# The first batch of a fused attention and Fourier kernel: the keys' half of a pair's memory and its scores in turn, the values' half last

## The chip, the cores and the metric

The kernel runs on one core of one Trainium2 chip. The metric is the device time of one execution in microseconds (us); lower is better. Three runs of the kernel before took 980.9, 981.11 and 982.27 us, median 981.11. Besides there is one profiled execution, whose trace is read below. TensorE is PE in the views, VectorE is DVE, ScalarE is ACT, GpSimd is POOL, and SP is the engine that issues the DMAs.

## The reference

Inputs are q, k, v of 8 batches x 8 heads x 576 tokens x 64, phi of 8 x 8 x 576 x 32, and two feed-forward weights of 512 x 2048 and 2048 x 512. Cut to what matters:

```python
a = softmax(phi, axis=2)                      # pooling weights per token
k_m = einsum('bhsm,bhsd->bhmd', a, k)         # 32 key memories per head
v_m = einsum('bhsm,bhsd->bhmd', a, v)         # 32 value memories per head
attn = softmax(q @ k_m.T / 8)                 # scores of 576 tokens over 32 memories
x = (attn @ v_m), heads side by side          # 576 x 512 per batch
u = x + real(fft(fft(x, axis=1), axis=2))     # Fourier mix over tokens and features
un = (u - mean) / sqrt(var + 1e-6)
out = u + relu(un @ w_ch1) @ w_ch2
```

## The kernel before

Heads are handled in pairs, four pairs (`NG`) per batch. For a pair, `pair_memory` makes on TensorE the product of keys and pooling weights (columns 0 to 63 of a PSUM tile `pm`) and of values and pooling weights (columns 64 to 127); VectorE multiplies both by a mask `mk` into `kmf` (in `share`) and `vmf`. `pair_scores` multiplies queries by `kmf` into a PSUM tile `psc`, makes the softmax on VectorE with the exponential on ScalarE, and writes sums and differences of tokens as float16 high and low parts into `aeo` (the low part of the first rows, on VectorE, is marked `s{b}_{g}`). `values` takes the products of `vmf` with the feature cosines `vt` (PSUM tiles `pv`, result `vh`), and `spectrum` those of `aeo` with the token cosines `ct` (PSUM tiles `pa`, result `at`). `mix_m` (PSUM tile `pp_t`, lines L600 to L640) and `mix_x` (`px_t`, from the transposed attention `attnT`) give rows of u in `uring`; `norm_chunk` normalises them, transposes them on TensorE for the first chunk (`unring`), and the feed-forward follows in chunks of 256 rows, 17 in all, each of 8 parts (`NW`) of the weights. PSUM tiles of all these steps but the feed-forward's `ph` and `po` share a pool of four buffers (`psg`).

The first chunk is different: its weights arrive as 64-bit floats and are converted on chip while they are first used (`ffn1_direct` into `ph`, `ffn2_direct` into `po`, float32 matmuls). A conversion (`to_f32`) is one pass on ScalarE (L808) and on VectorE a shift (L810) and two fused passes (L811, L821). For the keys in the list `LP`, the last one is instead a shift on VectorE (L816) and an integer add on POOL (L819). `split_w1` then makes two float16 parts. A square with its sum (L830) gives a scale.

Order: a scheduler places the instructions of each engine by its own timeline, so program order is not the order on the engine. `issue_after` holds an instruction behind a marked one, where both are on one engine; `GATE1` and `GATE2` name the marks that hold the conversion of w1's and w2's eight parts. `un1` is VectorE's normalisation of the second tile, `uh0` ScalarE's copy into `unring`. `high_priority` lets the scheduler place an instruction earlier. All loads go through SP in the order of issue; parts of the first batch's pairs are in tiles that later hold something else (`stg`, `w2s`), and pair 2's keys and values share bytes with w2's first converted part. `keep_busy` runs matmuls on zeros to keep TensorE's clock up.

Of the kernel before, what the change touches and what calls it, by code (L numbers as in the profile page):

```python
# [10 lines left out]
F32 = mybir.dt.float32  # L11
# [5 lines left out]
ALU = mybir.AluOpType  # L17
# [23 lines left out]
STEPS = 2  # L41
NX = 2
KEEP = [8, 18, 0, 0, 22, 4, 3]
GATE1 = [[]] + [["un1", "uh0"]] * 7
GATE2 = [["un1", "uh0"]] * 8
NA = 2
NAH = 1
KP = [1]
# [3 lines left out]
UW = UB * DM  # L52
EB = 14
L2 = [2, 4, 6]
LP = ["2_0", "2_2", "2_4", "2_6"]
W1_STAGE = ["w4", "w6", "s1", "w6", "s1", "s2", "s1", "x"]
W2_STAGE = ["b10", "b14", "s2", "b10", "b14", "x", "s2", "s1"]

# [74 lines left out]
def kernel(  # L133
# [72 lines left out]
    def tiny(tag, n, bufs=2):  # L206
        if tag not in rings:
            rings[tag] = [taken[0], 0]
            taken[0] += n * bufs
        o, i = rings[tag]  # L210
        rings[tag][1] += 1
        o += i % bufs * n
        assert taken[0] <= 400, taken
        return scratch[:, o : o + n]
# [52 lines left out]
    def groups():  # L267

        last = [None]

        def mm(out, lhsT, rhs, start, stop):
            with tc.issue_after(last[0].ins) if start and last[0] is not None else nullcontext():
                m = nc.tensor.matmul(out, lhsT=lhsT, rhs=rhs, start=start, stop=stop)  # L273
            if stop:
                last[0] = marks["pe"] = m

        return mm
# [56 lines left out]
    def pooling_weights(b):  # L334
# [28 lines left out]
        for g in range(2):  # L363
# [6 lines left out]
                et[:, g].rearrange("p l t c -> p (l t) c"), elt.rearrange("p l c -> p (l c)"), False, f"et_{b}_{g}"  # L370
            )

    def pair_memory(b, g, r, vmf, ivs):

        n = f"{b}_{g}"
        kv = r[:, :KV].rearrange("p (t w c) -> p t w c", t=NST, w=2)
        q = r[:, KV:]
        if b < NX:
            pm = psg.tile([P, 512], F32, tag="g", name=f"pm_{n}")
            mm = groups()  # L380
            for w in range(2):
                for t in range(NST):
                    mm(
                        pm[:, w * 64 : w * 64 + 64],
                        lhsT=kv[:, t, w, :],
                        rhs=et32[:, g // 2, t, 64 * (g % 2) : 64 * (g % 2) + 64],
                        start=(t == 0),
                        stop=(t == NST - 1),
                    )
            kmf = share[:, g * 64 : g * 64 + 64] if b == 0 else tiny("kmf", 64, 2)  # L390
            nc.vector.tensor_tensor(out=kmf, in0=pm[:, 0:64], in1=mk[:, 0:64], op=ALU.mult)
            nc.vector.tensor_tensor(
                out=vmf[:, g],
                in0=pm[:, 64:128].unsqueeze(1).to_broadcast([P, 2, 64]),
                in1=mk[:, 0:64].unsqueeze(1).to_broadcast([P, 2, 64]),
                op=ALU.mult,
            )
            return q, None, kmf, 1.0 / 8.0
        am = tiny("am", 3, 1)
        for w in range(2):  # L400
            nc.scalar.activation(
# [490 lines left out]
    def background():  # L892
# [3 lines left out]
        for b in range(B):  # L896
# [5 lines left out]
            pooling_weights(b)  # L902
            yield (nt if half_made is None else half_made), 0
            if b == 0:
                for g in range(NG):
                    mem[g] = pair_memory(b, g, first[g], vmf, ivs)
            for step in range(NG + 2):
                if step < NG and b > 0:
                    r = load_pair(b, step)
                if step >= 2 and b > 0:  # L910
                    pair_transpose(b, step - 2, ahl.pop(step - 2), attnT)
                if 0 <= step - 1 < NG:
                    ahl[step - 1] = pair_scores(b, step - 1, *mem.pop(step - 1), aeo)
                    yield (nt if half_made is None else half_made), 0
                if step < NG and b > 0:
                    mem[step] = pair_memory(b, step, r, vmf, ivs)
                    yield (nt if half_made is None else half_made), 0
            vbd, vh, isg, igx, isq = values(b, vmf, ivs)
# [30 lines left out]
        while True:  # L949
            yield n_tiles, 0  # L950

    nc.sync.dma_start(out=mk, in_=mk_d)
    load_phi(0)
    keep_busy(KEEP[0])
    first = [load_pair(0, 0)]
# [145 lines left out]
```

## Time and profile before

| quantity | value |
|---|---|
| median of 3 runs | 981.11 us |
| profiled execution, device time | 980.04 us |
| its span in the trace | 978.2 us |
| TensorE busy in the span | 937.8 us |
| VectorE busy in the span | 570.7 us |

The span begins with the first instruction and ends with the last; the device time also has 1.84 us around it. The page gives busy times and groups of instructions; the timeline gives instructions in order of time, merged where they follow one another (count behind the x), with the idle time in front in brackets; a window is a stretch of time with each engine's busy time in it. A row of matmuls in float32 counts each matmul twice.

### The profile page before, as it was taken

Reading aid. Unit: us, or ns where it says so; the run is one execution under the profiler, and the core shown is the slowest. Engines: PE = TensorE matmul, PEld = TensorE weight load, DVE = VectorE, ACT = ScalarE, POOL = GpSimd, SP = SyncE. Lnnn points to the kernel's source line nnn. Section 1 sums busy time; section 2 is a strip of 40 time slices with the busy share of each in tenths; the row PEclk is TensorE's granted clock in tenths of the full one; section 3 lists DMA queues with packets and bytes.
Section 4 is the critical chain, followed back from the end, with each engine's and each line's share of the span. In section 5 each row is a group of like instructions: output and inputs, shape, how many; then the busy total and the mean of one; then the engine's idle time right before and its main releaser. Section 6 shows DMA issues by size and latency. Waiting matters only on the chain.

```text
span 978.2 us, 18885 instructions
## 1 busy us (share of the span) xinstructions
PE 937.8 (96%) x7753; PEld 664.3 (68%) x7753; DVE 570.7 (58%) x1301; ACT 456.0 (47%) x910; POOL 229.9 (23%) x249
## 2 busy tenths in 40 slices
PE   9388898989999999999999999999999999999998
PEld 6256577666687667676767776767677667666664
DVE  3889958757655765776623666657655765311111
ACT  2455448695555544755431645565545543401110
POOL 1213324334221422333120223123311321300000
PEclk9699999999999999999999999999999999999999
DMA  9706564064225430465111632164214310210000
GB/s 351 282 7 265 180 173 131 1 140 122 62 50 99 116 88 29 88 127 122 39 23 36 122 107 68 44 120 122 69 44 86 79 26 29 44 44 1 23 22 22
DMA packets 115959, 88.08 MB, mean 90 GB/s; under 512 B 100385, under 2 KB 100385, under 8 KB 113825
## 3 DMA queue, kind: packets, MB, share of 16 engines
q1 hardware_dynamic: 115872, 86.87, 34.0%
q8 instruction: 61, 1.00, 0.5%
q14 instruction: 26, 0.20, 0.1%
HBM read 58.15 MB, written 9.44 MB: 69 GB/s over the span
## 4 chain that ended last, share of the span: by engine, by line
PE 82%; DVE 8%; ACT 4%; DMA 2%; issue 2%; POOL 1%; SPq 0%; DVEq 0%; POOLq 0%; ACTq 0%
PE po L765 34%; PE ph L273 33%; PE pm L273 4%; PE pp_t L273 3%; PE psc L273 2%; PE px_t L273 1%; PE pa L585 1%; DVE w1t L821 1%; DVE w2s L811 1%; PE po L729 1%; POOL scratch L678 1%; DMA rawt<-in_raw 1%; PE pf L343 1%; DVE w1t L811 1%; DVE uring L654 0%
## 5 line engine op out<-in xcount | busy, mean ns | idle before, releaser
L273 PE MATMUL ph<-unring,w1t 128*128 128x256 f16 x3264 | 389.0, 273 | 2.7 <-DMA unring<-ud 2.7
L765 PE MATMUL po<-w2s,hring 128*128 128x512 f16 x1632 | 378.6, 379 | 0.0
L273 PEld LDWEIGHTS <-w1t 128*128 128x128 f16 x3264 | 314.6, 98 | 65.8 <-DMA unring<-ud 3.2
L765 PEld LDWEIGHTS <-hring 128*128 128x128 f16 x1632 | 156.6, 98 | 158.0 <-issue 0.4
L756 DVE SCALAR_TENSOR_TENSOR hring<-ph,hring 128x512 f16<-128x512 f32 x136 | 93.0, 685 | 154.7 <-ACT hring L755 154.3
L755 ACT ACTIVATE hring<-ph 128x512 f16<-128x512 f32 x136 | 80.2, 590 | 168.3 <-PE ph L273 167.9
L501 POOL TENSOR_TENSOR aring<-aring,scratch 128x384 f32<-128x384 f32 x28 | 24.4, 870 | 202.2 <-DVE scratch L499 201.3
L678 POOL TENSOR_TENSOR scratch<-scratch,small 128x1 f32<-128x1 f32 x36 | 25.0, 700 | 155.6 <-DVE scratch L677 132.1
L273 PEld LDWEIGHTS <-stg 128*128 128x128 f16 x1152 | 44.9, 98 | 10.3 <-POOL stg L418 1.3
L495 ACT ACTIVATE aring<-aring,scratch 128x384 f32<-128x384 f32 x24 | 14.7, 612 | 70.4 <-DVE aring L494 70.4
L699 POOL TENSOR_TENSOR ud<-un,ud 128x1024 f16<-128x1024 f32 x17 | 37.5, 2203 | 29.9 <-ACT ud L698 29.9
L273 PE MATMUL pp_t<-vh,at 128*128 128x255 f16 (+3 forms) x288 | 36.6, 273 | 2.4 <-ACT at L600 1.5
L273 PE MATMUL pm<-et,stg 128*128 128x64 f16 (+1 forms) x780 | 37.0, 199 | 1.3 <-POOL stg L418 1.2
L418 POOL TENSOR_TENSOR stg<-rawt,stg 128x640 f16<-128x640 f32 x12 | 17.8, 1487 | 81.9 <-ACT rawt L417 81.9
L485 DVE TENSOR_REDUCE scratch<-psc 128x12 f32<-128x384 f32 x32 | 17.7, 552 | 32.6 <-PE psc L273 17.5
L640 DVE SCALAR_TENSOR_TENSOR share<-pp_t,scratch,small 128x257 f32<-128x257 f32 (+1 forms) x48 | 21.1, 480 | 25.3 <-ACT small L637 25.3
L729 PE MATMUL po<-w2s,hring 128*128 128x512 f32 x64 | 30.3, 600 | 4.8 <-ACT hring L715 2.9
L520 ACT CAST aeo<-eo 128x384 f16<-128x384 f32 x30 | 15.3, 511 | 41.4 <-DVE eo L517 41.2
L513 DVE TENSOR_TENSOR eo<-aring 128x128 f32<-128x128 f32 x29 | 30.8, 1063 | 5.6 <-POOL aring L511 5.6
L654 DVE SCALAR_TENSOR_TENSOR uring<-px_t,scratch,share 128x256 f32<-128x256 f32 (+1 forms) x80 | 33.9, 475 | 0.2
L777 DVE SCALAR_TENSOR_TENSOR uring<-po,small,uring 128x512 f32<-128x512 f32 x34 | 24.0, 741 | 16.5 <-PE po L765 16.5
L511 POOL TENSOR_TENSOR aring<-aring 128x128 f32<-128x128 f32 x56 | 32.7, 603 | 2.1
(240 smaller groups left out, 1232.6 us busy)
## 6 DMA issues: line engine op xcount, KB each, us to landing
rawt<-in_raw SPq DMA_DIRECT2D x15, 640.0 KB, 5.1
stg<-in_raw SPq DMA_DIRECT2D x15, 640.0 KB, 4.1
out<-uring SPq DMA_DIRECT2D x36, 256.0 KB, 2.3
stg<-in_w SPq DMA_DIRECT2D x7, 1024.0 KB, 5.7
rawt<-in_raw SPq DMA_DIRECT2D x15, 384.0 KB, 3.1
stg<-in_raw SPq DMA_DIRECT2D x15, 384.0 KB, 3.1
phs<-in_raw SPq DMA_DIRECT2D x32, 160.0 KB, 5.2
w2s<-in_w SPq DMA_DIRECT2D x4, 1024.0 KB, 9.8
```

The source lines that it names most:

```text
L273: m = nc.tensor.matmul(out, lhsT=lhsT, rhs=rhs, start=start, stop=stop)
L501: eng.tensor_tensor(out=a, in0=a, in1=sm.unsqueeze(2).to_broadcast([P, 12, M]), op=ALU.mult)
L511: eng.tensor_tensor(out=a2[:, i : i + 4], in0=a[:, 0:4], in1=a[:, 4:8], op=op)
L513: nc.vector.tensor_tensor(out=eo[:, 1:3, 0], in0=ap[:, 1:3, 0], in1=ap[:, 1:3, 1], op=ALU.add)
L654: nc.vector.scalar_tensor_tensor(out=u[rows, hs], in0=px[rows, hs], scalar=igx[rows], in1=tm[rows, w * NJ + half : w * NJ + half + 256], o ...
L678: nc.gpsimd.tensor_tensor(out=rs, in0=rs, in1=half, op=ALU.pow)
L699: marks[f"ul{c}"] = nc.gpsimd.tensor_tensor(out=ud[:, 1], in0=un, in1=ud[:, 0], op=ALU.subtract)
L729: nc.tensor.matmul(po[t], lhsT=h[:, f, t], rhs=w[:, f], start=(j == 0 and f == 0), stop=(j == NW - 1 and f == UB - 1),)
L755: nc.scalar.activation(h[:, 0], phv, AF.Relu)
L756: nc.vector.scalar_tensor_tensor(out=h[:, 1], in0=phv, scalar=0.0, in1=h[:, 0], op0=ALU.max, op1=ALU.subtract)
L765: nc.tensor.matmul(po[t], lhsT=hs[j][:, lh, f * 2 + t], rhs=w2s[:, j * UB + f, lw, :], start=(j == 0 and f == 0 and i == 0), stop=(j == NW ...
L777: nc.vector.scalar_tensor_tensor(out=u, in0=po[t], scalar=cout if c else 0.5, in1=u, op0=ALU.mult, op1=ALU.add)
```

## The change

Three things change in the first batch. The memories of a pair are made in two halves by `memory_f32`: the keys' half of pair g, then the scores of pair g - 1, and after all scores the values' half of the four pairs, each in a PSUM tile of its own. The load of the masks gets a high priority. `GATE1` and `GATE2` of part 0 are `s0_3`, the last scores' mark on VectorE (part 0 of w1 had no mark, part 0 of w2 had `un1` and `uh0`), and `LP` is empty.

```diff
@@ -41,8 +41,8 @@
 STEPS = 2
 NX = 2
 KEEP = [8, 18, 0, 0, 22, 4, 3]
-GATE1 = [[]] + [["un1", "uh0"]] * 7
-GATE2 = [["un1", "uh0"]] * 8
+GATE1 = [["s0_3"]] + [["un1", "uh0"]] * 7
+GATE2 = [["s0_3"]] + [["un1", "uh0"]] * 7
 NA = 2
 NAH = 1
 KP = [1]
@@ -52,7 +52,7 @@
 UW = UB * DM
 EB = 14
 L2 = [2, 4, 6]
-LP = ["2_0", "2_2", "2_4", "2_6"]
+LP = []
 W1_STAGE = ["w4", "w6", "s1", "w6", "s1", "s2", "s1", "x"]
 W2_STAGE = ["b10", "b14", "s2", "b10", "b14", "x", "s2", "s1"]
 
@@ -370,32 +370,41 @@
                 et[:, g].rearrange("p l t c -> p (l t) c"), elt.rearrange("p l c -> p (l c)"), False, f"et_{b}_{g}"
             )
 
-    def pair_memory(b, g, r, vmf, ivs):
-
-        n = f"{b}_{g}"
+    def memory_f32(b, g, r, vmf, parts):
+
         kv = r[:, :KV].rearrange("p (t w c) -> p t w c", t=NST, w=2)
-        q = r[:, KV:]
-        if b < NX:
-            pm = psg.tile([P, 512], F32, tag="g", name=f"pm_{n}")
-            mm = groups()
-            for w in range(2):
-                for t in range(NST):
-                    mm(
-                        pm[:, w * 64 : w * 64 + 64],
-                        lhsT=kv[:, t, w, :],
-                        rhs=et32[:, g // 2, t, 64 * (g % 2) : 64 * (g % 2) + 64],
-                        start=(t == 0),
-                        stop=(t == NST - 1),
-                    )
+        pm = psg.tile([P, 512], F32, tag="g", name=f"pm_{b}_{g}_{len(kept)}")
+        kept.append(pm)
+        mm = groups()
+        for w in parts:
+            for t in range(NST):
+                mm(
+                    pm[:, w * 64 : w * 64 + 64],
+                    lhsT=kv[:, t, w, :],
+                    rhs=et32[:, g // 2, t, 64 * (g % 2) : 64 * (g % 2) + 64],
+                    start=(t == 0),
+                    stop=(t == NST - 1),
+                )
+        kmf = None
+        if 0 in parts:
             kmf = share[:, g * 64 : g * 64 + 64] if b == 0 else tiny("kmf", 64, 2)
             nc.vector.tensor_tensor(out=kmf, in0=pm[:, 0:64], in1=mk[:, 0:64], op=ALU.mult)
+        if 1 in parts:
             nc.vector.tensor_tensor(
                 out=vmf[:, g],
                 in0=pm[:, 64:128].unsqueeze(1).to_broadcast([P, 2, 64]),
                 in1=mk[:, 0:64].unsqueeze(1).to_broadcast([P, 2, 64]),
                 op=ALU.mult,
             )
-            return q, None, kmf, 1.0 / 8.0
+        return kmf
+
+    def pair_memory(b, g, r, vmf, ivs):
+
+        n = f"{b}_{g}"
+        kv = r[:, :KV].rearrange("p (t w c) -> p t w c", t=NST, w=2)
+        q = r[:, KV:]
+        if b < NX:
+            return q, None, memory_f32(b, g, r, vmf, range(2)), 1.0 / 8.0
         am = tiny("am", 3, 1)
         for w in range(2):
             nc.scalar.activation(
@@ -902,17 +911,24 @@
             pooling_weights(b)
             yield (nt if half_made is None else half_made), 0
             if b == 0:
+
+                for g in range(NG + 1):
+                    if g < NG:
+                        km = memory_f32(b, g, first[g], vmf, [0])
+                        mem[g] = first[g][:, KV:], None, km, 1.0 / 8.0
+                    if g > 0:
+                        ahl[g - 1] = pair_scores(b, g - 1, *mem.pop(g - 1), aeo)
                 for g in range(NG):
-                    mem[g] = pair_memory(b, g, first[g], vmf, ivs)
-            for step in range(NG + 2):
-                if step < NG and b > 0:
+                    memory_f32(b, g, first[g], vmf, [1])
+            for step in range(NG + 2) if b > 0 else ():
+                if step < NG:
                     r = load_pair(b, step)
-                if step >= 2 and b > 0:
+                if step >= 2:
                     pair_transpose(b, step - 2, ahl.pop(step - 2), attnT)
                 if 0 <= step - 1 < NG:
                     ahl[step - 1] = pair_scores(b, step - 1, *mem.pop(step - 1), aeo)
                     yield (nt if half_made is None else half_made), 0
-                if step < NG and b > 0:
+                if step < NG:
                     mem[step] = pair_memory(b, step, r, vmf, ivs)
                     yield (nt if half_made is None else half_made), 0
             vbd, vh, isg, igx, isq = values(b, vmf, ivs)
@@ -949,7 +965,8 @@
         while True:
             yield n_tiles, 0
 
-    nc.sync.dma_start(out=mk, in_=mk_d)
+    with tc.high_priority(1000):
+        nc.sync.dma_start(out=mk, in_=mk_d)
     load_phi(0)
     keep_busy(KEEP[0])
     first = [load_pair(0, 0)]
```

What TensorE has in a row, from the first memory to the value spectrum (`pm` are memories, `psc` scores, the first digit behind them the pair). Before:

```order
L273 MATMUL pm_0_215<-et,rawt 128x64 x10
L273 MATMUL pm_1_228<-et,stg 128x64 x10
L273 MATMUL pm_2_241<-et,w2s 128x64 x10
L273 MATMUL pm_3_254<-et,w2s 128x64 x10
L273 MATMUL psc_0_267<-share,rawt 128x64 x6
L273 MATMUL psc_1_291<-share,stg 128x64 x6
L273 MATMUL psc_2_315<-share,w2s 128x64 x6
L273 MATMUL psc_3_339<-share,w2s 128x64 x6
```

And now, TensorE, the same place:

```order
L273 MATMUL pm_0_4_215<-et,rawt 128x64 x5
L273 MATMUL pm_1_5_222<-et,stg 128x64 x5
L273 MATMUL psc_0_229<-share,rawt 128x64 x6
L273 MATMUL pm_2_6_253<-et,w2s 128x64 x5
L273 MATMUL psc_1_260<-share,stg 128x64 x6
L273 MATMUL pm_3_7_284<-et,w2s 128x64 x5
L273 MATMUL psc_2_291<-share,w2s 128x64 x6
L273 MATMUL psc_3_315<-share,w2s 128x64 x6
L273 MATMUL pm_0_8_339<-et,rawt 128x64 x5
L273 MATMUL pm_1_9_346<-et,stg 128x64 x5
L273 MATMUL pm_2_10_353<-et,w2s 128x64 x5
L273 MATMUL pm_3_11_360<-et,w2s 128x64 x5
```

The first score has moved in front of the memories of pairs 2 and 3, and the values' halves behind all scores.

VectorE between the last scores and the first mix, before (`aeo` are the scores' low parts, `at` the spectrum's low part, `share` the mix):

```order
L522 SCALAR_TENSOR_TENSOR aeo<-aeo,small,un 128x4x32
L522 SCALAR_TENSOR_TENSOR aeo<-aeo,small,eo 128x4x32
L597 SCALAR_TENSOR_TENSOR at<-pa_0_0_413,at 128x2x145
L597 SCALAR_TENSOR_TENSOR at<-pa_0_1_423,at 128x2x145
L597 SCALAR_TENSOR_TENSOR at<-pa_1_0_433,at 128x2x145
L597 SCALAR_TENSOR_TENSOR at<-pa_1_1_443,at 128x2x145
L640 SCALAR_TENSOR_TENSOR share<-pp_t_482,scratch,small 128x257 x2
```

And now, VectorE, the same place (line numbers behind the change are some 9 higher; `vh` is the value spectrum's low part):

```order
L531 SCALAR_TENSOR_TENSOR aeo<-aeo,small,eo 128x4x32
L819 TENSOR_SCALAR w1t<-w1t 128x1024
L819 TENSOR_SCALAR w2s<-w2s 128x1024
L820 SCALAR_TENSOR_TENSOR w1t<-w1t 128x1024
L820 SCALAR_TENSOR_TENSOR w2s<-w2s 128x1024
L830 SCALAR_TENSOR_TENSOR w1t<-w1t 128x1024
L830 SCALAR_TENSOR_TENSOR w2s<-w2s 128x1024
L576 SCALAR_TENSOR_TENSOR vh<-pv_0_387,vh 128x512
L576 SCALAR_TENSOR_TENSOR vh<-pv_1_388,vh 128x512
L606 SCALAR_TENSOR_TENSOR at<-pa_0_0_417,at 128x2x145
L606 SCALAR_TENSOR_TENSOR at<-pa_0_1_427,at 128x2x145
```

Six conversion passes now stand between the last scores and the spectrum's low part, and `vh`, which stood among the scores, is behind them.

ScalarE now, from the first exponential (L504) on (L817 is the conversions' pass on ScalarE, L517 and L529 are casts of the scores, L547 is a square over `vmf`):

```order
L504 ACTIVATE aring<-aring 128x384 x2
L517 CAST ahring<-aring 128x5x64
L817 ACTIVATE w1t<-w1t 128x1024
L529 CAST aeo<-eo 128x12x32
L504 ACTIVATE unring<-unring 128x384 x2
L817 ACTIVATE w2s<-w2s 128x1024
L517 CAST ud<-aring 128x5x64
L547 ACTIVATE share,scratch<-vmf 128x4x64
```

The two passes of part 0's conversions stand among the softmaxes; before, w1's stood in front of the first exponential and w2's behind the norm.

## Rows read from the trace of the kernel before

**Rows 1.** The page, part 1: busy time of an engine, its share of the span, instructions.
```profile
PE 937.8 (96%) x7753; PEld 664.3 (68%) x7753; DVE 570.7 (58%) x1301; ACT 456.0 (47%) x910; POOL 229.9 (23%) x249
```

**Rows 2.** Windows of 20 us: stretch, its length, busy time of PE, PEld, DVE, ACT, POOL.
```profile
60.00:80.00 20.00, 14.61 (x81) 10.80 (x81) 18.83 (x22) 14.19 (x21) 6.00 (x2) 1.00 0.36 132
...
100.00:120.00 20.00, 18.07 (x63) 11.40 (x63) 19.97 (x29) 8.65 (x18) 8.12 (x3) 1.00 0.60 184
```

**Rows 3.** Timeline 8 to 30 us: start, duration, engine, line, what, count [idle before].
```profile
9.21 0.33 SPq L952 DMA_DIRECT2D small<-in_mk  x1
...
13.71 2.34 PE L273 MATMUL pm<-et,rawt 128*128 128x64 f32 x20
...
18.29 0.23 DVE L391 TENSOR_TENSOR share<-pm,small 128x64 f32<-128x64 f32 x1 [4.44 <-PE pm L273]
...
20.68 1.14 ACT L808 ACTIVATE w1t<-w1t 128x1024 f32<-128x1024 f32 x1 [7.16 <-DMA w1t<-in_w]
...
22.59 1.50 PE L273 MATMUL psc<-share,rawt 128*128 128x64 f32 x12
...
24.13 0.56 DVE L485 TENSOR_REDUCE scratch<-psc 128x12 f32<-128x384 f32 x1 [0.32 <-PE psc L273]
```

**Rows 4.** DMA view 0 to 60 us: tile, queue, count, KB, us from issue to landing.
```profile
small<-in_mk SPq DMA_DIRECT2D x1, 34.0 KB, 9.0
```

**Rows 5.** Timeline 26 to 46 us, VectorE's conversion, values and last scores.
```profile
26.67 1.21 DVE L821 SCALAR_TENSOR_TENSOR w1t<-w1t 128x1024 uint32<-128x1024 uint32 x1
...
41.31 1.27 DVE L567 SCALAR_TENSOR_TENSOR vh<-pv,vh 128x512 f16<-128x512 f32 x2
...
45.01 0.75 DVE L522 SCALAR_TENSOR_TENSOR aeo<-aeo,small,eo 128x128 f16<-128x128 f16 x1
```

**Rows 6.** Timeline 45 to 54 us: the spectrum, the transposes' copies and the first mix.
```profile
45.82 0.42 PE L577 MATMUL pa<-ct,aeo 128*128 128x290 f16 x1 [9.62 <-DVE aeo L522]
...
49.00 1.72 DVE L597 SCALAR_TENSOR_TENSOR at<-pa,at 128x290 f16<-128x290 f32 x4 [3.23 <-ACT at L596]
...
50.37 1.48 PE L273 MATMUL pp_t<-vh,at 128*128 128x257 f16 x12
...
51.42 1.33 ACT L265 COPY attnT<-pt_attnT 128x640 f16<-128x640 f16 x2
...
53.15 0.88 DVE L640 SCALAR_TENSOR_TENSOR share<-pp_t,scratch,small 128x257 f32<-128x257 f32 x2 [2.43 <-ACT small L637]
```

**Rows 7.** Windows of 1 us in the spectrum; the number behind POOL's is TensorE's granted clock.
```profile
46.00:47.00 1.00, 1.00 (x7) 0.79 (x6) 0.00 (x0) 0.00 (x0) 0.00 (x0) 0.50 0.00 0
49.00:50.00 1.00, 1.00 (x21) 1.00 (x19) 1.00 (x3) 1.00 (x4) 0.00 (x0) 1.00 0.00 0
```

**Rows 8.** Waits of PE from 60 us to the end: who for whom, us, times, longest.
```profile
PE pa L577 <- DVE aeo L522: 3.3, 1, 3.3
PE po L729 <- ACT hring L715: 2.9, 1, 2.9
...
PE px_t L273 <- DVE share L640: 2.1, 1, 2.1
PE po L729 <- issue: 1.9, 1, 1.9
...
PE ph L712 <- ACT unring L695: 0.7, 1, 0.7
```

**Rows 9.** Timeline 60 to 70 us: POOL's add and VectorE's shift beside it.
```profile
63.51 2.73 POOL L819 TENSOR_TENSOR w2s<-w2s 128x1024 int32<-128x1024 int32 x1 [5.13 <-issue]
63.89 2.90 DVE L810 TENSOR_SCALAR w2s<-w2s 128x1024 int32<-128x1024 int32 x1
```

**Rows 10.** Groups by line, whole run: busy, mean ns of one, idle before.
```profile
L816 DVE TENSOR_SCALAR w2s<-w2s 128x1024 uint32<-128x1024 uint32 x2 | 1.3, 670 | 0.0
```

**Rows 11.** Groups by line on POOL, whole run: the integer adds.
```profile
L819 POOL TENSOR_TENSOR w2s<-w2s 128x1024 int32<-128x1024 int32 x2 | 6.1, 3058 | 5.1 <-issue 5.1
L819 POOL TENSOR_TENSOR w2s<-stg,w2s 128x1024 int32<-128x1024 int32 x2 | 5.8, 2900 | 19.9 <-DVE scratch L321 10.0 <-DVE w2s L811 9.9
```


## Prediction

> **What bounds the kernel now.** I read the page first: TensorE is busy 937.8 of 978.2 us [rows 1], so all engines but TensorE matter only where TensorE stands still, and that is 40.4 us in all. The table of windows says where: from 200 us to 900 it hardly stops, while 60 to 80 us has 14.6 of 20 busy and 100 to 120 us 18.1, with VectorE at 18.8 and 20.0 of 20 [rows 2]. So a change of the first batch is worth what it takes out of TensorE's early waits, at most, and VectorE is what those waits are for. Then the timeline of the first 54 us. The pairs' memories start on TensorE at 13.71, but the first score only at 22.59, since all eight half-memories are in front of it; VectorE's softmax starts at 24.13 [rows 3]. The masks, issued at 9.21, land 9.0 us later, at 18.2 [rows 3, 4], and the first masking runs at 18.29 [rows 3]. From 24.13 VectorE works through four softmaxes, the conversion of w1's first part and the value spectrum, until the last `aeo` ends at 45.76 [rows 3, 5]; the spectrum on TensorE waited 9.62 us for it [rows 6]. Last the view of waits behind 60 us [rows 8] and the timeline of VectorE beside POOL [rows 9].
>
> **The change part by part.**
>
> *Scores earlier.* In the new TensorE order two key halves precede the first score. A pair's two halves took 2.34 us [rows 3], so two halves end at 13.71 + 2.34 = 16.05; the score takes 1.50 [rows 3], and the softmax can start at 17.6 instead of 24.1. This needs the masks by 16. They are now queued behind two pairs and a half instead of four pairs and `ct`, 3.4 MB by the tile sizes instead of 5.3; landing at 18.2 for 5.3 puts them at 12 to 14 (estimate). If they still came at 18.2, 2.3 us would be lost. No matmul is added: the same 80 are in another order, the value halves last (about 24.4 to 29.1).
>
> *VectorE up to the last `aeo`.* Before: 45.76 - 24.13 = 21.6 us, in which it is hardly idle. Out of it go the two long conversion passes, 1.2 each [rows 5], and the two passes on `vh` (1.27, [rows 5]), which now stand behind it: 17.9 left. In come two key and four value masks, 6 x 0.25 (0.23 in rows 3) = 1.5, and some 1.0 of waiting, since scores now arrive every 2.7 us (one score and one half). So T, the end of `aeo`, is 17.6 + 17.9 + 1.5 + 1.0 = 38.0, against 45.8: 7.8 earlier, give or take 2.
>
> *What comes behind `aeo`.* The gate puts six passes in front of `vh` and `at` on VectorE: a shift of 0.67 ([rows 10], same shape) and two of 1.21 [rows 5], for w1 and for w2: 2 x 3.1 = 6.2. Then `vh` 1.3 and `at` 1.7 [rows 5, 6]: `at` ends at T + 9.2. Before it ended at 50.72, that is T + 5.0, with VectorE idle 3.23 in front [rows 6]: the idle time covers half of the conversions, the rest is on the path. The first `vh` pass also gives back the PSUM buffer that the third `pa` waits for, so TensorE stalls inside the spectrum; that hides behind VectorE. From the end of `at` to the first mix on VectorE (L640) took 53.15 - 50.72 = 2.4 us, filled with copies on ScalarE; now three copies of transposes (0.67 each, [rows 6]) follow instead of two, so 2.9. The mix starts at 38.0 + 9.2 + 2.9 = 50.1, against 53.15: **3.0 us gained** out of 7.8. Bounds: 1 and 6. The norm and the start of the direct feed-forward follow with the same steps, so they move by the same 3.0.
>
> *w2's first part converted early, TensorE's order behind the norm.* Before, the first `po` waited 2.9 for `hring`, whose copy stands behind conversions on ScalarE, and the first `ph` 0.7 for `unring` [rows 8]. Now one conversion fewer is in that ScalarE queue, and TensorE has the second mix (`pp_t` takes 1.48, [rows 6]) and part of the third in front of `po`. I take both waits as gone: **3.6**. Bounds 1 and 3.6.
>
> *POOL's integer adds gone.* Four adds on POOL, 3.06 and 2.90 us on the mean [rows 11], go; each is replaced by making a shift of 0.67 [rows 10] a fused pass of 1.21 [rows 5] on VectorE: 4 x 0.54 = 2.2 us more there. But beside such an add a VectorE shift of 0.7 took 2.90 [rows 9], 2.2 longer. If each add held VectorE so, 8.8 go, and VectorE has 6.6 less to do in a stretch where it is full [rows 2]. On TensorE that shows as two waits: 2.1 for `share` and 1.9 before a later `po` [rows 8], 4.0. Of the two I count 1.6, since VectorE is full and new waits will stand elsewhere. Bounds 0 and 6.6.
>
> *Loads.* w2's first part is now in front of `vt`; `vt` is first read in the value spectrum, behind 30 us, and the queue is past it by then. Nothing.
>
> *Sum.* 3.0 + 3.6 + 1.6 = 8.2 of TensorE's standing still. The rest of the program is as full as before and moves ahead as a whole, except where batch 1 has its own chain (`pa` waits 3.3, [rows 8]); I leave that as it is. The profiled execution took 980.04 (span 978.2 and 1.84 around it); 980.04 - 8.2 = 971.8. It lies 1.1 under the median of the runs, 981.11, so the median to be expected is 972.9.
>
> **The rivals.**
>
> *A, half clock through the mixes.* The granted clock was 0.50 (1.2 GHz) at 46 to 47 us, after TensorE had waited, and 1.00 (2.4 GHz) at 49 to 50, after it had worked on `pa` without a break [rows 6, 7]. Now the stall for the PSUM buffer splits `pa` in two. If the clock stays low behind it, the transposes and `pp_t` (about 1.5 each before, `pp_t` in rows 6) take twice as long on the path: 3.0 more, 975.9. Against it: the second `pa` burst, transposes and `pp_t` again follow without a break. The Trainium skill ("TensorE: Matmul & The Clock Gate", section "What's actually happening") says that "the default state is throttled, and activity releases the throttle"; the trace agrees with its 0.50 and 1.00 on either side of 48 us, and by that rule the split would bring this case about.
>
> *B, the gate holds only VectorE.* In ScalarE's order the two first passes of the conversions stand between the softmaxes' exponentials and casts, the second one where it overwrites half of pair 2's tile and so waits for its value half. Each takes 1.14 [rows 3]. If VectorE has nothing else then, T is 2.3 later: 975.2. Against it: VectorE has two other pairs to work on by then.
>
> *C, given back at batch 1.* If `pa` of batch 1, which already waits 3.3 [rows 8], hangs on loads or ScalarE and not on TensorE's progress, the wait grows by what was gained: 981.
>
> *D, slower.* The six conversion passes are stretched by POOL, as the shift of 2.90 was [rows 9]: 6 x 2.9 = 17.4 instead of 6.2. The mix starts 11.2 later, at 61.3, 8.2 behind before; only the 3.6 come back, so 981.1 + 8.2 - 3.6 = 985.7. It decides from a stretch of 6.6 (3.0 + 3.6), 1.1 a pass. Against it: POOL has only the last pairs' small subtractions there, no integer add.
>
> *E, all of VectorE's time counts.* If the whole 6.6 reaches TensorE instead of 1.6, 967.9.
>
> **How the numbers follow.** Forecast 0.54, own range 969 to 977. A 0.12, B 0.12, C 0.08, D 0.06, E 0.08. 0.2% (2.0 us) is about what a measurement of this kernel can tell from no change: under 979.1 is faster, over 983.1 slower. Forecast, A, B and E are faster: 0.86; C is the same: 0.08; D slower: 0.06. For 8 in 10 I leave out C and D above and a little of E below: 966 to 979. The likeliest is 972.9; A and B lie above it and E below, so I keep it at 973.
>
> **What would show it.** Right: the first score at 16 to 17 us, the masks landed by 15; the last `aeo` at 36 to 40; the first mix at 48 to 52; no wait of over 1 us of the first `po` on `hring`; no VectorE shift over 1 us between 55 and 120; TensorE's idle time 31 to 34 us instead of 40.4. Wrong: `aeo` behind 41 (B or late masks); `pp_t` at clock 0.50 (A); conversion passes of over 2 us (D); a wait of `pa` in batch 1 well over 3.3 (C).

## The result, and the profile after

The changed kernel takes 967.23 us (median of 4 runs, 966.45 to 967.69) against 981.37 us for the kernel before on the same chip: ratio 0.9854, 95% interval [0.9837, 0.9871]. That is 14.1 us faster; 8.2 were forecast (973), and 967.2 lies inside the range of 966 to 979, near its lower end. The profiled execution took 967.11 us, its span is 965.2, against 980.04 and 978.2. Of the experiments below, one execution of e3 took 1229 us and one of e5 3301; the ratios leave both out, the medians count them (without them 975.2 and 974.0).

Part 1 of the page of after, answering [rows 1]:

```profile
PE 937.8 (97%) x7753; PEld 664.4 (69%) x7753; DVE 564.0 (58%) x1301; ACT 456.3 (47%) x910; POOL 214.1 (22%) x245
```

TensorE does the same work in the same 937.8 us; its standing still has gone from 40.4 to 27.4 us. Windows of after, answering [rows 2]:

```profile
60.00:80.00 20.00, 20.00 (x88) 12.95 (x87) 20.00 (x32) 11.06 (x21) 0.00 (x0) 1.00 0.75 290
80.00:100.00 20.00, 17.42 (x69) 12.10 (x68) 20.00 (x37) 12.50 (x25) 6.94 (x3) 1.00 0.48 148
100.00:120.00 20.00, 20.00 (x86) 13.50 (x85) 12.78 (x22) 5.51 (x10) 0.00 (x0) 1.00 0.65 209
```

TensorE's idle time was 18.2, 5.4, 0.9 and 1.9 us in the stretches that end at 60, 80, 100 and 120 us, and is 12.0, 0.0, 2.6 and 0.0. Behind 120 us it was 14.1 and is 12.9. So all but 1.2 of the 13.0 us come from the first 120.

The timeline of after, 5 to 20 us, and the masks' DMA, answering [rows 3, 4]:

```profile
6.20 0.71 SPq L969 DMA_DIRECT2D small<-in_mk  x1
14.81 0.22 DVE L391 TENSOR_TENSOR share<-pm,small 128x64 f32<-128x64 f32 x1 [1.13 <-PE pm L273]
15.73 1.50 PE L273 MATMUL psc<-share,rawt 128*128 128x64 f32 x12
17.27 0.56 DVE L494 TENSOR_REDUCE scratch<-psc 128x12 f32<-128x384 f32 x1 [1.12 <-PE psc L273]
...
small<-in_mk SPq DMA_DIRECT2D x1, 34.0 KB, 8.1
```

The masks land at 14.3, the first score begins 6.9 us earlier than before. VectorE from the last scores to the mix, answering [rows 5, 6]:

```profile
36.23 0.76 DVE L531 SCALAR_TENSOR_TENSOR aeo<-aeo,small,eo 128x128 f16<-128x128 f16 x1
36.91 0.68 DVE L819 TENSOR_SCALAR w1t<-w1t 128x1024 int32<-128x1024 int32 x1
...
41.52 1.21 DVE L830 SCALAR_TENSOR_TENSOR w2s<-w2s 128x1024 uint32<-128x1024 uint32 x1
42.65 1.28 DVE L576 SCALAR_TENSOR_TENSOR vh<-pv,vh 128x512 f16<-128x512 f32 x2
43.85 1.58 DVE L606 SCALAR_TENSOR_TENSOR at<-pa,at 128x290 f16<-128x290 f32 x4
48.05 0.88 DVE L649 SCALAR_TENSOR_TENSOR share<-pp_t,scratch,small 128x257 f32<-128x257 f32 x2 [2.62 <-ACT small L646]
```

The last `aeo` ends at 36.99 (45.76 before), the six passes run behind it without a gap, and the mix begins at 48.05 (53.15 before). TensorE's clock in the spectrum, answering [rows 7], in windows:

```profile
38.00:40.00 2.00, 2.00 (x15) 1.80 (x16) 2.00 (x3) 1.61 (x4) 0.00 (x0) 0.50 1.04 386
40.00:41.00 1.00, 1.00 (x16) 0.92 (x14) 1.00 (x2) 0.00 (x0) 0.00 (x0) 0.99 0.90 328
```

The granted clock rises from 0.50 (1.2 GHz) to full (2.4 GHz) at 40 us and stays there up to about 158 us. Up to 40 us TensorE had worked without a gap from 35.29 on, on transposes, `pv` and then `pa`. TensorE's waits from 60 us on, answering [rows 8]:

```profile
PE pa L586 <- DVE aeo L531: 3.2, 1, 3.2
PE pp_t L273 <- ACT at L609: 3.0, 1, 3.0
PE ph L273 <- DMA unring<-ud: 2.4, 1, 2.4
PE ph L721 <- DVE w1t L830: 1.9, 1, 1.9
PE po L738 <- ACT hring L724: 0.6, 1, 0.6
```

The first three stand behind 150 us. What is left of the first chunk's waits is 1.9 us for a pass on w1t and 0.6 of a later `po`. The timeline of POOL, VectorE and TensorE there, answering [rows 9]:

```profile
89.10 4.20 POOL L708 TENSOR_TENSOR ud<-un,ud 128x1024 f16<-128x1024 f32 x1 [4.92 <-ACT ud L707]
...
91.50 2.89 DVE L830 SCALAR_TENSOR_TENSOR w1t<-stg,w1t 128x1024 uint32<-128x1024 uint32 x1
...
94.65 3.69 PE L721 MATMUL ph<-unring,w1t 128*128 128x256 f32 x16 [1.93 <-DVE w1t L830]
```

The pass, 1.21 us otherwise, takes 2.89 beside the end of POOL's subtraction of 4.20. The shifts on VectorE, one line by its tile, answering [rows 10, 11] (durations are least, median, most):

```profile
L819 DVE TENSOR_SCALAR w1t<-w1t x9: 420/675/694, 36.9 to 107.0; 128x1024 int32<-128x1024 int32 x7, 128x512 int32<-128x512 int32 x2
L819 DVE TENSOR_SCALAR w2s<-w2s x9: 407/680/694, 37.5 to 109.7; 128x1024 int32<-128x1024 int32 x7, 128x512 int32<-128x512 int32 x2
```

No shift is held any more.

### The profile page after: what moved, and what is told of

Its sections match the earlier page's. It is cut to its first block, busy times and chain, and to the rows that moved or that the text cites. A ratio compares the mean times of both kernels' runs of the same rounds, so it can differ in the third digit from the quotient of the medians.

```text
span 965.2 us, 18877 instructions
## 1 busy us (share of the span) xinstructions
PE 937.8 (97%) x7753; PEld 664.4 (69%) x7753; DVE 564.0 (58%) x1301; ACT 456.3 (47%) x910; POOL 214.1 (22%) x245
## 4 chain that ended last, share of the span: by engine, by line
PE 86%; DVE 7%; DMA 2%; ACT 2%; issue 1%; POOL 1%; DVEq 0%; POOLq 0%; ACTq 0%
PE po L774 35%; PE ph L273 35%; PE pm L273 3%; PE pp_t L273 3%; PE psc L273 2%; DMA phs<-in_raw 2%; PE px_t L273 1%; PE po L738 1%; PE ph L721 1%; PE pa L594 1%; PE keep L251 1%; DVE w1t L830 1%; PE pf L343 1%; DVE w2s L820 1%; DVE uring L663 1%
## 5 line engine op out<-in xcount | busy, mean ns | idle before, releaser
L687 POOL TENSOR_TENSOR scratch<-scratch,small 128x1 f32<-128x1 f32 x36 | 22.7, 632 | 174.2 <-DVE scratch L686 155.6
L504 ACT ACTIVATE aring<-aring,scratch 128x384 f32<-128x384 f32 x24 | 14.7, 611 | 57.6 <-DVE aring L503 57.6
L529 ACT CAST aeo<-eo 128x384 f16<-128x384 f32 x30 | 15.3, 511 | 42.8 <-DVE eo L526 42.7
L273 PEld LDWEIGHTS <-at 128*128 128x128 f16 (+1 forms) x288 | 29.0, 104 | 8.5 <-ACT at L609 3.2
L721 PE MATMUL ph<-unring,w1t 128*128 128x256 f32 x128 | 30.5, 381 | 1.9 <-DVE w1t L830 1.9
```

The source lines that it names most:

```text
L687: nc.gpsimd.tensor_tensor(out=rs, in0=rs, in1=half, op=ALU.pow)
L721: nc.tensor.matmul(ph, lhsT=w[:, k, f * P : (f + 1) * P], rhs=unTs[0][:, k], start=(k == 0), stop=(k == NK - 1))
```

## The experiments

Three edits make up the change: the turns (with the masks' load), the two gates, and the empty `LP` ("no adds"). All eight combinations were timed. "Idle" and "busy" are TensorE's, in us, in the one profiled execution; "busy" rises where matmuls run at half clock, since all eight kernels have the same 7753. The medians were taken on different chips, so kernels are compared by the ratios, each of which was taken against before on its own chip.

| turns | gates | no adds | run | median us | ratio [95%] | idle to 120 us | idle after | busy |
|---|---|---|---|---|---|---|---|---|
| | | | before | 981.37 | 1 | 26.3 | 14.1 | 937.8 |
| | | x | e1_noadds | 983.41 | 1.0020 [1.0009, 1.0032] | 21.7 | 17.4 | 941.6 |
| | x | | e2_gates | 984.03 | 1.0021 [1.0011, 1.0032] | 23.7 | 14.6 | 943.9 |
| | x | x | e12_gates_noadds | 973.75 | 0.9919 [0.9906, 0.9931] | 20.0 | 12.4 | 941.2 |
| x | | | e3_turns | 975.65 | 0.9936 [0.9923, 0.9950] | 17.5 | 12.6 | 943.6 |
| x | | x | e11_turns_noadds | 977.64 | 0.9960 [0.9944, 0.9976] | 19.0 | 17.4 | 940.4 |
| x | x | | e4_adds_back | 976.31 | 0.9942 [0.9928, 0.9956] | 17.6 | 13.3 | 943.6 |
| x | x | x | after | 967.23 | 0.9854 [0.9837, 0.9871] | 14.5 | 12.9 | 937.8 |

Two things stand in it. The turns are worth the same with and without the other two: 0.64% (6.3 us) from before to e3, 0.65% from e12 to after. The gates and the missing adds are worth 0.81% (7.9 us) without the turns and 0.82% with them, but only as a pair: either alone leaves the time the same or makes it 0.6 to 2.4 us longer.

**e1_noadds** and **e2_gates**, one edit each, on the kernel before.

```diff
-LP = ["2_0", "2_2", "2_4", "2_6"]
+LP = []
```

> The kernel before with nothing changed but the list of keys whose last conversion pass is an integer add on POOL, which is empty. Theory M (the gain of 14 us is a sum of two about independent parts: scores earlier, 5 to 6 us in front of the norm, and VectorE freed of POOL's adds, 4 to 6 us behind it): 975 to 977.5, the first mix on VectorE still at 53.1 us, no VectorE shift over 2 us between 60 and 120. Theory R (the adds are the whole matter and the scores' lead is eaten up by the conversions): 967 to 970. Theory S (all of it is the scores' lead): 981.

```diff
-GATE1 = [[]] + [["un1", "uh0"]] * 7
-GATE2 = [["un1", "uh0"]] * 8
+GATE1 = [["s0_3"]] + [["un1", "uh0"]] * 7
+GATE2 = [["s0_3"]] + [["un1", "uh0"]] * 7
```

> The kernel before with the two gates of the first weights' part alone: both conversions held behind the last scores. Theory M: VectorE loses 2.4 us of passes in front of the spectrum and gets some 6 behind it, of which 3 to 4 lie in its idle time; first mix 0 to 2 us earlier, 979 to 981.5. Theory R: 981. Theory S' (holding the conversions is what gives the scores their lead): 975 to 977.

Both came out slower, by 0.20% and 0.21%, which no theory had, though each took idle time out of the first 120 us: 4.7 and 2.6. In e1's profiled execution this went into 3.3 more behind 120 us and 3.8 more of busy time. TensorE in the kernel before, timeline at the first `po`:

```profile
67.01 3.67 PE L729 MATMUL po<-w2s,hring 128*128 128x512 f32 x8 [2.88 <-ACT hring L715]
```

and in e1, with two windows of the stretch:

```profile
67.13 6.71 PE L729 MATMUL po<-w2s,hring 128*128 128x512 f32 x8 [2.81 <-ACT hring L715]
...
66.00:68.00 2.00, 0.87 (x1) 0.50 (x2) 2.00 (x3) 2.00 (x4) 0.00 (x0) 0.60 0.04 8
68.00:70.00 2.00, 2.00 (x4) 0.82 (x3) 2.00 (x3) 0.38 (x2) 0.00 (x0) 0.50 0.00 0
```

The same wait at the same place, and the same `po`, take 3.0 us more in e1: behind the wait the clock was granted at 0.50, in before at 1.00.

In e2 the first mix did not begin up to 2 us earlier but 3.0 later. Timeline of e2, POOL and VectorE in front of it:

```profile
48.58 2.41 POOL L819 TENSOR_TENSOR w2s<-w2s 128x1024 int32<-128x1024 int32 x1 [4.38 <-PE pt_attnT L264]
...
49.12 2.95 DVE L821 SCALAR_TENSOR_TENSOR w1t<-w1t 128x1024 uint32<-128x1024 uint32 x1
...
56.16 0.88 DVE L640 SCALAR_TENSOR_TENSOR share<-pp_t,scratch,small 128x257 f32<-128x257 f32 x2 [3.32 <-ACT small L637]
```

The gate on w2's first part moves that part's POOL add, which in before stood at 63.51 [rows 9], in front of the mix. There it holds a pass of w1's conversion for 2.95 us instead of 1.21, with half of `at` still behind that pass. With the add gone (e12, below) the pass takes 1.21 and the mix begins 2.5 us earlier. This is one way in which the gates need the missing adds.

**e3_turns** and **e4_adds_back**: after with the old gates and the old `LP`, and after with the old `LP` alone.

```diff
# e3, in after
-GATE1 = [["s0_3"]] + [["un1", "uh0"]] * 7
-GATE2 = [["s0_3"]] + [["un1", "uh0"]] * 7
-LP = []
+GATE1 = [[]] + [["un1", "uh0"]] * 7
+GATE2 = [["un1", "uh0"]] * 8
+LP = ["2_0", "2_2", "2_4", "2_6"]
# e4, in after
-LP = []
+LP = ["2_0", "2_2", "2_4", "2_6"]
```

> The changed kernel with the old gates and the old list of POOL adds, so that only the order of memories and scores and the early masks are left of the change. Theory M: first softmax at 17.3 us, first mix 4 to 6 us earlier than 53.1, 974 to 977. Theory R: 979 to 981. Theory S: 967 to 970.

> The changed kernel with the old list of POOL adds. Theory M: first mix at 48 us as in the changed kernel (one add is made earlier, beside the spectrum, so up to 2 us later), then VectorE held beside the adds again: 970.5 to 974. Theory R: 978 to 981. Theory S: 967.

e3 came out as theory M had it; e4 lies between its theories M and R. The adds alone, put back, cost 0.88%, 8.6 us. Timeline of e4, POOL, VectorE and TensorE at 88 to 105 us:

```profile
88.53 4.35 POOL L708 TENSOR_TENSOR ud<-un,ud 128x1024 f16<-128x1024 f32 x1 [2.01 <-ACT ud L707]
94.10 3.31 POOL L828 TENSOR_TENSOR w2s<-w2s 128x1024 int32<-128x1024 int32 x1 [1.21 <-DVE w2s L820]
...
91.41 2.56 DVE L820 SCALAR_TENSOR_TENSOR w2s<-w2s 128x1024 int32<-128x1024 int32 x1
95.08 3.41 DVE L830 SCALAR_TENSOR_TENSOR w1t<-stg,w1t 128x1024 uint32<-128x1024 uint32 x1
...
98.55 6.11 PE L721 MATMUL ph<-unring,w1t 128*128 128x256 f32 x16 [4.09 <-DVE w1t L830]
```

Two passes of 1.21 are held, one beside the subtraction and one beside the add; the `ph` that needs the second waits 4.09 us, 1.93 in after, and then takes 6.11 instead of 3.69 us at half clock. e2 has the same picture six us later (passes of 2.55 and 3.41, a wait of 4.08, a `ph` of 6.09). So this is what the gates meet while the adds are there. In e4 TensorE also ran the first mix at half clock (0.50 from 46 to 50 us), and VectorE's part of the mix began at 49.42, 1.4 later than in after: rival A's case, in another kernel.

**e11_turns_noadds** and **e5_w2late**: after with both gates put back, and with w2's alone.

```diff
# e11, in after
-GATE1 = [["s0_3"]] + [["un1", "uh0"]] * 7
+GATE1 = [[]] + [["un1", "uh0"]] * 7
# e11 and e5, in after
-GATE2 = [["s0_3"]] + [["un1", "uh0"]] * 7
+GATE2 = [["un1", "uh0"]] * 8
```

> The changed kernel with the old gates: memories and scores in turn, early masks, no POOL adds; w1's first conversion is not held and w2's is held behind the norm. Theory C (the parts' gains in idle time add up, and what differs besides is the time at half clock): TensorE's idle time 27 to 31 us, device time 967 to 972 with no fall of the clock behind 50 us, up to 975 with one. Theory G (the gates are what makes the POOL adds' removal pay): 974.5 to 976 with idle time over 33.

> After, with the gate on w2's first part alone put back to where it was behind the norm; w1's gate, the turns and the missing POOL adds stay. Theory (w2's part converted early is what takes away the first po's wait for hring, and with it the fall of the granted clock behind that wait): the first po waits 2.5 to 3.0 us for hring at 58 to 62 us again, the granted clock falls to 0.50 behind it, and the time is that of the kernel with both gates put back, 975 to 979. Rival (w1's part held behind the scores is what counts, since it leaves VectorE to the softmaxes): no fall, the mix half a us earlier than in after for want of three passes, 966 to 969.

e11 took 977.64, above both of its theories, and its idle time of 36.4 us is far from the 27 to 31 of theory C. e5 took 974.05 us (ratio 0.9914 [0.9900, 0.9928]); the expected 975 to 979 is missed by 1 us. Its mechanism is there. Timeline of e5, TensorE:

```profile
60.90 5.40 PE L738 MATMUL po<-w2s,hring 128*128 128x512 f32 x8 [2.81 <-ACT hring L724]
```

The first `po`, with no wait in front in after, waits 2.81 again, and its eight matmuls take 5.40 instead of some 3.7. The mix began at 47.10, 0.95 earlier than in after, as the rival had it, and that did not count. The clock was 0.50 at 62 to 64 us. So w2's early conversion carries a little over half of the gates' share: 0.60% of the 1.06% between after and e11.

**e12_gates_noadds**, the pair without the turns, in the old order and with the masks where they were.

```diff
# in before
-GATE1 = [[]] + [["un1", "uh0"]] * 7
-GATE2 = [["un1", "uh0"]] * 8
-LP = ["2_0", "2_2", "2_4", "2_6"]
+GATE1 = [["s0_3"]] + [["un1", "uh0"]] * 7
+GATE2 = [["s0_3"]] + [["un1", "uh0"]] * 7
+LP = []
```

> The kernel before with both gates and without the POOL adds, in the old order of memories and scores and with the masks where they were. Theory (the gate on w2's first part takes away the first po's wait for hring, the missing adds take away the ph's wait for a held VectorE pass, and only both together leave the clock alone; the turns are a gain of their own): about 9 us faster than before, 970 to 974, TensorE idle 31 to 34 us, no wait of po on hring near 65 us, no wait of ph on a conversion pass over 2 us near 100 us, granted clock 1.00 from 50 to 150 us. Rival (the gain of the two edits needs the turns, because in the old order the six conversion passes stand on the path to the mix): 978 to 983, with the first mix two to three us later than before, at 55 to 56.

973.75 us, as the theory had it. Timeline of e12, TensorE and VectorE:

```profile
67.60 1.98 PE L729 MATMUL po<-w2s,hring 128*128 128x512 f32 x4
...
53.67 0.88 DVE L640 SCALAR_TENSOR_TENSOR share<-pp_t,scratch,small 128x257 f32<-128x257 f32 x2 [2.41 <-ACT small L637]
```

No wait in front of the first `po`, the longest for a conversion pass is 1.9, and the clock is 1.00 from 48 to 158 us. Here the gates delay the mix by 0.5 us (53.67, 53.15 before), and not by 2 to 3. Idle time 32.4 us, as expected (31 to 34).

**e9_noadds_fill** and **e10_turns_fill**: e1 and e3 with 11 matmuls on zeros, 2.5 us, between the first part's `ph` and `po`, to fill the wait. They add nothing to the output. `m` is the last of the part's `ph` matmuls.

```diff
+        if j == 0:
+            pt = psg.tile([P, 512], F32, tag="g", name="fill")
+            kept.append(pt)
+            with tc.issue_after(m.ins):
+                for _ in range(11):
+                    m = nc.tensor.matmul(pt, lhsT=zeros[:, :P], rhs=zeros, start=True, stop=True)
+            marks["fill"] = m
```

> The kernel before with the empty list of POOL adds, as in e1, and 11 matmuls on zeros (512 columns, 0.22 us each at full clock, 2.4 us in all) between the first part's ph and po, where TensorE waited 2.8 us for hring and its clock then stood at 0.50 to about 73 us. They add nothing to the output. Theory C (clock: e1 loses its gain to a stretch at half clock behind this wait): the granted clock stays 1.00 from 60 to 80, the po of 67 us take 3.7 instead of 6.7, 978 to 981, 2.5 to 4 us under e1's 983.4. Theory V (e1 gains nothing because VectorE is not what TensorE waits for): 983 to 986, with the matmuls' time added or hidden.

> Memories and scores in turn with the old gates and POOL adds, as in e3, and the same 11 matmuls on zeros between the first part's ph and po. Theory C: no half clock at 60 to 67 us, 971 to 974, 2 to 4 under e3's 975.7. Theory V: 975 to 978.

Timeline of e9, TensorE:

```profile
64.78 2.54 PE L721 MATMUL fill<-uring 128*128 128x512 f16 x11
67.80 3.70 PE L736 MATMUL po<-w2s,hring 128*128 128x512 f32 x8 [0.48 <-ACT hring L715]
```

The clock held: `po` takes 3.70, not 6.71. Yet e9 took 985.4 us (ratio 1.0038 [1.0025, 1.0051]), 0.18% more than e1, and e10 977.97 (0.9965 [0.9953, 0.9976]), 0.29% more than e3; the first pair of intervals overlaps, the second just doesn't. So theory V fits both, not theory C. Half clock came elsewhere: at 123 to 126 and 191 to 198 us in e9, at 115 to 119, 163 to 167 and 180 to 184 in e10, and TensorE was busy for 944.9 and 944.8 us, 2.5 of them the fill. The fill keeps the clock up at its own place and saves nothing over the kernel.

**e6_masklate**, after with the masks' load at its old priority.

```diff
-    with tc.high_priority(1000):
-        nc.sync.dma_start(out=mk, in_=mk_d)
+    nc.sync.dma_start(out=mk, in_=mk_d)
```

> After, with the masks' load in its old place behind the pairs. Theory of the prediction (masks landing at 18.2 hold the first masking, and so the softmax, by 2.3 us): masks land at 17.5 to 18.5, the first score near 18.5 instead of 15.7, first mix 1 to 2.8 us later than in after, 968 to 970. Rival (the chain from the scores to the mix has so much slack in ScalarE and VectorE that a late start is caught up): the mix within 0.5 us of after, 967.

968.13 us (0.9859 [0.9847, 0.9872]), no difference from after within the intervals. Timeline and DMA view of e6, then two windows:

```profile
5.80 0.47 SPq L968 DMA_DIRECT2D small<-in_mk  x1
...
small<-in_mk SPq DMA_DIRECT2D x1, 34.0 KB, 7.6
...
94.00:96.00 2.00, 1.03 (x5) 0.96 (x6) 2.00 (x4) 0.00 (x0) 0.00 (x0) 1.00 0.58 111
96.00:98.00 2.00, 2.00 (x7) 1.62 (x6) 2.00 (x5) 0.42 (x2) 0.00 (x0) 0.56 1.38 216
```

The run does not answer its question: without the priority the load was issued at 5.80, even earlier, and landed at 13.4. With the scores in turn the scheduler brings the masks forward by itself; the priority does nothing. By the way it shows the clock once more: behind the same wait of 1.9 us for the same pass as in after, it fell to half at 96 us, and in after it did not. Nor need that be a property of e6: over its four executions the mean granted clock goes from 0.989 to 0.993, and the two at 0.991 and 0.993 took 967.58 and 966.68 us, those at 0.989 took 968.68 (the profiled one) and 969.15.

**e8_w2at** and **e7_at**, tries at a better kernel: after with w2's first conversion held behind the spectrum's low part, and with both.

```diff
# e8 and e7
-                nc.vector.scalar_tensor_tensor(
+                marks[f"at{b}"] = nc.vector.scalar_tensor_tensor(
-GATE2 = [["s0_3"]] + [["un1", "uh0"]] * 7
+GATE2 = [["at0"]] + [["un1", "uh0"]] * 7
# e7 as well
-GATE1 = [["s0_3"]] + [["un1", "uh0"]] * 7
+GATE1 = [["at0"]] + [["un1", "uh0"]] * 7
```

> The changed kernel with w2's first conversion held on VectorE behind the last low part of the spectrum instead of behind the last scores, so that three passes (3.1 us) less stand in front of vh and at. Theory M (these passes are on the path to the first mix): the mix starts 2 to 3 us earlier, at 45.5, and 965 to 966.5 follows. Theory H (hidden: TensorE's low clock and ScalarE's copies end as late): 967 to 968. Against both, the passes now in front of the mix may delay it again: 968 to 970.

> After, with the conversions of both first parts held behind the spectrum's low part (at) instead of the last scores. Theory (each three passes on VectorE that leave the stretch between the last scores and the mix bring the mix forward; with w2's three it came forward and the time was 964.6): mix another 2 us or so earlier, at 44 to 46, but the first feed-forward matmul needs w1's three passes and its split behind the mix; 962 to 966. Rival (w1's conversion becomes the last thing the first ph waits for): a wait of the first ph of 3 us or more on w1t, 967 to 971.

e8 took 964.57 us (0.9829 [0.9816, 0.9842]), the fastest of all, 0.25% below after, its interval reaching just into that of after, and a little below the 965 to 966.5 of theory M. Timeline of e8, VectorE:

```profile
45.51 1.22 DVE L830 SCALAR_TENSOR_TENSOR w2s<-w2s 128x1024 uint32<-128x1024 uint32 x1
46.65 0.87 DVE L649 SCALAR_TENSOR_TENSOR share<-pp_t,scratch,small 128x257 f32<-128x257 f32 x2
```

w2's three passes now run where VectorE had stood idle in front of the mix (2.62 us in after), which begins 1.4 us earlier, not 2 to 3. e7 took 973.56 us (0.9927 [0.9910, 0.9944]; runs from 972.8 to 977.7): neither theory. Its mix began at 47.42, not at 44 to 46: the fifth of six passes ended only then, so VectorE and no longer the copies set it. And the loss was not a wait of the first `ph`; the longest, in the profiled run of 977.68 us, timeline of TensorE:

```profile
113.94 1.11 PE L326 MATMUL pt_e<-identf,phs 128*128 128x128 f32 x4 [5.67 <-DVE phs L322]
```

A transpose of batch 1's pooling weights, queued on TensorE between two parts of the first chunk, waits 5.67 us for VectorE. The same trace shows why VectorE is late, timeline of POOL, SP and ScalarE:

```profile
89.61 11.29 POOL L708 TENSOR_TENSOR ud<-un,ud 128x1024 f16<-128x1024 f32 x1 [4.01 <-ACT ud L707]
...
102.97 1.02 SPq L807 DMA_DIRECT2D stg<-in_w  x1
...
108.72 1.12 ACT L817 ACTIVATE w2s<-stg 128x1024 f32<-128x1024 f32 x1 [10.40 <-DMA stg<-in_w]
```

POOL's subtraction, 4.20 us in after and 2.13 at the median of its 17 executions in this run, takes 11.29 beside VectorE, which works through its passes without a gap. SP holds the transposing DMA of its result until 100.93 (93.33 in after), and the next load of weights is in line behind it: 102.97 instead of 95.36. ScalarE waits 10.40 us for this load (2.43 in after), VectorE then 7.39 for ScalarE, and the pooling weights stand behind that on VectorE. So the loss reaches TensorE by way of a load. Whether it does so in the other executions of e7, and whether the moved passes bring it about, is not shown: they have no trace.

## Why the prediction came out as it did

*The sum against the rows.* The forecast was too careful by 5.7 us (972.9, measured 967.23). In the profiled executions TensorE's busy time is the same before and after, so all of the gain there is idle time: 6.2 us up to 60 us, where 3.0 were forecast; 5.6 from 60 to 120, where 3.6 + 1.6 = 5.2 were; 1.2 behind 120, where nothing was. That is 4.8 more than the 8.2. The remaining 0.9 is the distance from profile to median: 1.1 us before, which the forecast carried over, and 0.1 after. The idle time of 27.4 us lies below the 31 to 34 that were to show the forecast right. So the way was right, and the term that was mis-sized is the first, the way to the mix.

*First score, masks, last `aeo`.* Nearly right: the score at 15.73 for 16.05, the masks at 14.3 (12 to 14 were estimated), T 36.99 for 38.0. The masks came in time, but the priority was not what did it (e6).

*From `aeo` to the mix.* Right in kind, too small: `at` ended at T + 8.4 instead of T + 9.2 and the copies took 2.6 instead of 2.9, so the mix gained 5.1 us and not 3.0, inside the bounds of 1 and 6. Three small allowances all lay on the careful side: 1.0 up to T, of which 0.3 is the earlier first softmax and 0.4 less waiting than priced, then 0.8 and 0.3. The stall in the spectrum did not come where it was put, in front of the third `pa`: the four `pa` and the first two groups of transposes ran through, and the third group of transposes waited 1.7 for `vh`. It was hidden, as said. The turns by themselves, which e3 and e12 measure, are worth 6.3 us.

*w2's first part early.* Both waits went, 3.6, as forecast: the first `po` runs at 61.99 with nothing in front, behind the second and third mix.

*POOL's adds.* This is the term that was wrong in its nature. It was priced as 1.6 us (0 to 6.6) of two waits for VectorE, added to the rest. The waits, timeline of before (the first was not counted):

```profile
77.26 1.48 PE L273 MATMUL pp_t<-vh,at 128*64 128x257 f16 x12 [0.83 <-DVE scratch L232]
...
80.86 0.30 PE L273 MATMUL px_t<-vbdt,attnT 128*64 128x128 f16 x2 [2.13 <-DVE share L640]
...
107.51 1.96 PE L729 MATMUL po<-w2s,hring 128*128 128x512 f32 x4 [1.93 <-issue]
```

All three are gone in after, and also in e1, where only the adds went; most of the first two lies in the 5.4 us by which the idle time from 60 to 80 us fell. New waits of 1.9 and 0.6 came in their place, as the forecast had reckoned. VectorE's busy time fell by 5.4 from e4 to after, near the 6.6 priced. And yet the edit gains nothing by itself (e1, e11), while putting the adds back costs 8.6 us (e4), above the upper bound; in the profiled executions it is 9.3: 3.0 of idle time up to 120, 0.5 behind, and 5.8 of busy time at half clock. The sum of separate terms failed here: gates and adds priced apart gave 3.6 + 1.6 = 5.2, measured they give 7.9 together and less than nothing apart. That the idle time from 60 to 120 fell by 5.6, so near to 5.2, is in part luck.

*What the sum left out.* Outside rival A no half-clock stretch was priced, though waits of TensorE put more of them at risk. After in its profiled execution escaped them between 40 and 158 us and kept its 937.8 us of busy time, as before did; the other six kernels of the table were 2.6 to 6.1 us above it in theirs.

*Rivals.* A: no; the clock rose at 40 us and stayed up through the mixes. The rule of the Trainium skill that spoke for it ("TensorE: Matmul & The Clock Gate", section "What's actually happening") is not against that: TensorE's work from 35.29 us on had released the clock before the stall, which came behind `pa`. B: no, T came earlier, not later. C: no; `pa` of batch 1 waits 3.2, as before 3.3. D: no; the six passes took 0.68 and 1.21 each. In e2, where an add stood there, one of them took 2.95. E, "all of VectorE's time counts", 967.9, hit the time, but not for its reason: what was missing from the sum lay mostly in the first 60 us, in front of the stretch that E speaks of.

*What stays open.* Why the clock falls behind a wait in one kernel and not behind the same wait in another (e1 and before; e6 and after). It also differs between executions of one kernel: in 54 executions of before the mean granted clock lies between 0.978 and 0.989; the 22 at 0.981 or less took 982.4 us at the median, the 13 at 0.987 or more 980.6. The profiled one of before has 0.989, that of e1 0.984, but over all executions on their chip e1's median clock is 0.986 and that of before 0.983. So the busy time by which the profiled e1 lies above before belongs in part to the executions that were profiled, and that half clock is why e1 and e2 gain nothing is not shown; that after keeps more of the clock is, 0.991 to 0.993 in its four executions. The Trainium skill says on the same page and in the same section that the monitor behind the clock gate runs freely and isn't reset when a kernel starts; that would fit, but no run here tests it. Open is also how much of e1's, e2's, e4's, e5's and e11's loss comes from batch 1: in all five, and in e9, a float16 `po` at 180 to 192 us waits 3.5 us for a pass on w2s that has no such wait in before, e3, e12 and after. By which way the pair gains differs too: in the profiles, without the turns (before to e12) it is 8.0 less idle and 3.4 more busy time, with them (e3 to after) 2.6 and 5.8 less.

## What to carry to other kernels

Where two edits each remove one of two waits on the same chain, test them as a pair and alone: here neither alone gained anything and both gained 8 us. Beside a kernel's idle time read TensorE's busy time against that of the same matmuls before; a rise is half clock, and it can eat what the shorter waits gave. Read the granted clock of several executions, since one profile is one of them. Put work that nobody needs soon into the idle time just in front of the next link of the chain, as e8 did; e7, which put twice as much there, lost. When a conversion is moved, look at which engine its last step runs on: in e2 the moved step was a POOL add, which held VectorE in front of the mix.

## What the runs showed of the hardware

- A wait of 2.81 us of TensorE was followed by half clock and eight matmuls of 6.71 us together; one of 2.88 at the same place of another kernel by full clock and 3.67. A wait of 1.9 was followed by half clock in one kernel (e6) and not in another (after).
- Matmuls on zeros in such a wait held the clock there (`po` 3.70), and the kernel still had as much half clock in the end, at other places.
- A VectorE pass with two inputs, 1.21 us alone, took 2.89 and 2.56 beside a POOL subtraction of 4.2 to 4.4 us and 3.41 beside a POOL integer add of 3.31. In these rows it made next to no progress until POOL had ended: it ended 1.09 us behind POOL in after (94.39 and 93.30) and 1.09 and 1.08 in e4, and the shift of 2.90 in [rows 9], 0.68 alone, 0.55 behind. So what a held pass loses is about what is left of POOL's instruction when it begins. POOL is held as well: its subtraction of 2.13 at the median took 11.29 in e7 beside VectorE passes without a gap. The Trainium skill ("GPSIMD Engine Reference", section "8. Key points") says that GpSimd shares its SBUF interfaces with VectorE, with contention where VectorE's instruction has two inputs in SBUF or is in a 2-port mode; the trace agrees for the passes with two inputs, and whether the shift, with one input, was in such a mode no run here shows.
